# One store or two per 128-row output tile in place of four, in a memory-attention and two-layer kernel

## The chip, the cores and the metric

The kernel runs on one core of a Trainium2 chip. The metric is the device time of the whole program in microseconds, as the median of the timed runs of the same kernel on the same inputs. Smaller is better.

## The reference

Attention against 32 memory rows per head, then a gated layer, then a layer with a sigmoid-weighted activation. What is cut is only the random inputs.

```python
def _attn_ref(q, k, v, phi):            # q, k, v: (4, 8, 576, 64); phi: (4, 8, 576, 32)
    a = softmax of phi over the sequence
    k_m = np.einsum('bhsm,bhsd->bhmd', a, k)
    v_m = np.einsum('bhsm,bhsd->bhmd', a, v)
    attn = softmax of scale * q @ k_m.T over the memory rows
    return attn @ v_m

x = attn_out.transpose(0, 2, 1, 3).reshape(2304, 512)
x = ((x @ w_a) * (x @ w_b)) @ w_out              # d_ff 1536
h = x @ w_in                                     # d_ff 2048
return (h * (1.0 / (1.0 + np.exp(-1.702 * h)))) @ w_out2     # (2304, 512) float32
```

## The kernel before

The 2304 tokens are 4 batches of 576. A small planner (`Order`, L67 to L143) runs generators in an order that it works out from estimated costs, and each generator issues its instructions when it is resumed; the order on each engine is thereby fixed when the program is built. It plans TensorE, VectorE, ScalarE and GpSimd. Transfers that are issued from SyncE are not planned: they stand in SyncE's queue in the order in which the generators reach them.

Within a batch the tokens are held in a permuted order. A block is 32 tokens (`QP`), and a batch has 18 blocks (`QC`). The rows of the batch are seen as 32 groups of 18 consecutive rows; a block holds one row out of each group, so the 32 rows of a block stand 18 rows apart in memory. The first nine blocks of a batch (288 tokens, half a batch) hold the even rows of the groups, the last nine the odd rows. Row c of an even half is row 2c of each group.

The tail of the kernel is the second layer. `main` (L860) runs over eight groups of 256 hidden columns, and within a group over six units of 384 tokens: `gelu` (L773) makes the hidden values of a unit, `proj2` (L817) multiplies them into three tiles of 128 tokens by 512 output columns, 6 matmuls (L828) a tile. `proj2_out` (L838) adds a tile into `acc` in SBUF on VectorE (L844). In the last group it then calls `store` (L806) for the tile. A tile has four blocks; `store` goes over them one by one and issues one transfer a block on SyncE: 32 partitions of `acc` to 32 rows of the output, 2 KB each, 18 rows apart. 18 tiles of four blocks make 72 transfers (L815). Nothing writes a tile of `acc` after its store, and no later instruction but the end of the program waits for a store.

The half batch has nine blocks and a tile has four, so a tile can begin at any of the nine blocks, and some tiles reach over the end of a half.

Of the kernel before, what the change touches and what calls it, by code (L numbers as in the profile page):

```python
# [146 lines left out]
def tile_mem_attention_moe_moe2(  # L147
# [13 lines left out]
    nc = tc.nc  # L161

    w_a, w_b, w_o1, w_in, w_o2 = (w.bitcast(U32) for w in (w_a, w_b, w_o1, w_in, w_o2))
    B, H, S, D = q.shape
# [4 lines left out]
    P = 128  # L169
# [5 lines left out]
    QP = P // 4  # L175
    QC = S // QP
# [629 lines left out]
    def store(i, src):  # L806

        for t in range(i * P, (i + 1) * P, QP):
            b, r = divmod(t, S)
            e, c = divmod(r // QP, QC // 2)
            dst = out[b * S:(b + 1) * S, :].rearrange("(p c) e -> p c e", c=QC)
            nc.sync.dma_start(out=dst[:, 2 * c + e, :], in_=src[t - i * P:t - i * P + QP, :])  # L815

    def proj2(g, i):  # L817
        t0 = yield from weights("o2", g)
# [19 lines left out]
    def proj2_out(t, g, it, ps):  # L838
        dst = acc_o[:, it, :]
        t, _ = yield DVE, t, dve(512)  # L840
        if g == 0:
            nc.vector.tensor_copy(dst, ps[0])
        else:
            nc.vector.tensor_tensor(out=dst, in0=ps[0], in1=dst, op=ALU.add)  # L844
        bank_m.release(ps, t)
        if g == NG2 - 1:
            store(it, dst)
# [81 lines left out]
    with tc.manual_schedule():  # L929
# [15 lines left out]
        for n in range(NU):  # L945
            p = 10 + n if n >= NHG else 10 + PC * n
# [42 lines left out]
```

## Time and profile before

| | us |
|---|---|
| median of three timed runs | 832.27 |
| lowest and highest of them | 831.84, 833.02 |
| the profiled execution's own time | 829.86 |
| its span, from the first to the last instruction | 828.1 |
| TensorE busy | 808.0 |
| VectorE busy | 565.3 |
| ScalarE busy | 363.4 |
| GpSimd busy | 319.8 |

All rows come from one profiled execution. Its engines are PE (TensorE matmul), PEld (its weight loads), DVE (VectorE), ACT (ScalarE) and POOL (GpSimd); SPq is the queue of SyncE, which here only issues transfers. A transfer is made of packets that 16 DMA engines carry; a share of DMA is the mean busy share of these 16. The span is 1.76 us shorter than that execution's own time, and that time is 2.41 us under the median of the timed runs.

### The profile page before, as it was taken

The numbers are of one execution on the slowest core, as the hardware profiler recorded it, in microseconds if no ns is written. First come the engines' busy times: TensorE is split into PE (matmuls) and PEld (weight loads), VectorE is DVE, ScalarE is ACT, GpSimd is POOL, SyncE is SP. The second block draws the span as 40 slices with busy tenths as digits, with TensorE's granted clock in tenths as the row PEclk, the third lists the DMA queues.
The fourth block names the chain that finished last, engine by engine and source line by source line (L and its number), as shares of the span: only waits on it lengthen the run. The fifth ranks groups of instructions, "written<-read, shape, count | busy, mean of one in ns | idle before, by whom it ended". The sixth has DMA issues, their size and how long they took to land.

```text
span 828.1 us, 13746 instructions
## 1 busy us (share of the span) xinstructions
PE 808.0 (98%) x5290; PEld 743.5 (90%) x5290; DVE 565.3 (68%) x1020; ACT 363.4 (44%) x795; POOL 319.8 (39%) x294
## 2 busy tenths in 40 slices
PE   8999999999999999999999999999999999999996
PEld 7777788989999999999999899989898989999995
DVE  4988879997977969858498664846557384444342
ACT  4567777454445536436553333324233242322220
POOL 1212255643524426326675433424334161322120
PEclk9999999999999999999999999999999999999999
DMA  8866402240310301301022110201103000000134
GB/s 301 296 208 186 145 1 77 82 149 2 104 50 27 102 26 52 104 1 51 1 74 80 48 55 0 82 21 52 51 1 102 1 26 1 1 0 1 33 87 110
DMA packets 33025, 57.77 MB, mean 70 GB/s; under 512 B 3520, under 2 KB 15808, under 8 KB 32960
## 3 DMA queue, kind: packets, MB, share of 16 engines
q1 hardware_dynamic: 32128, 56.08, 21.6%
q10 hardware_dynamic: 832, 0.82, 0.3%
q8 instruction: 41, 0.67, 0.3%
q14 instruction: 24, 0.20, 0.1%
HBM read 52.17 MB, written 4.72 MB: 69 GB/s over the span
## 4 chain that ended last, share of the span: by engine, by line
PE 79%; DVE 10%; ACT 4%; issue 3%; DMA 2%; POOL 0%; SPq 0%; DVEq 0%; ACTq 0%
PE bank L828 23%; PE bank L787 22%; PE bank L731 13%; PE bank L698 13%; PE bank L659 2%; DVE dm L351 2%; DVE dm L347 1%; DMA raw<-in_moe_w_b_dram 1%; DVE dm L356 1%; PE bank L491 1%; PE bank L631 1%; DVE gr L714 1%; PE bank L531 1%; DVE acc L748 1%; PE bank L406 1%
## 5 line engine op out<-in xcount | busy, mean ns | idle before, releaser
L828 PE MATMUL bank<-wo,g 128*128 128x512 f32 x864 | 204.6, 390 | 0.2 <-POOL g L253 0.2
L253 POOL TENSOR_TENSOR g<-sg,g 128x384 fp32r<-128x384 f32 x95 | 102.8, 1084 | 226.9 <-ACT g L259 180.2
L828 PEld LDWEIGHTS bank<-wo,g 128*128 128x128 f32 x864 | 161.5, 188 | 31.5 <-POOL g L253 0.6
L800 DVE TENSOR_TENSOR sg<-bank,sg 128x384 f32<-128x384 f32 x96 | 53.4, 556 | 115.2 <-ACT sg L798 115.2
L798 ACT ACTIVATE sg<-bank 128x384 f32<-128x384 f32 x96 | 47.0, 489 | 177.7 <-PE bank L787 177.4
L844 DVE TENSOR_TENSOR acc<-bank,acc 128x512 f32<-128x512 f32 x126 | 86.8, 689 | 51.4 <-PE bank L828 51.3
L253 POOL TENSOR_TENSOR g<-gr,g 128x288 fp32r<-128x288 f32 x74 | 64.0, 867 | 135.5 <-ACT g L259 128.9
L787 PE MATMUL bank<-y,whl_b 128*128 128x384 f32 x576 | 105.0, 337 | 0.0
L787 PE MATMUL bank<-y,whl_a 128*128 128x384 f32 x576 | 104.2, 336 | 0.5 <-DVE sg L800 0.5
L787 PEld LDWEIGHTS bank<-y,whl_b 128*128 128x128 f32 x576 | 101.7, 188 | 1.9
L787 PEld LDWEIGHTS bank<-y,whl_a 128*128 128x128 f32 x576 | 100.7, 188 | 2.5 <-DVE sg L800 0.9
L731 PE MATMUL bank<-g,whl_a 128*128 128x288 f32 x576 | 82.9, 298 | 0.9 <-DVE gr L714 0.7
L731 PEld LDWEIGHTS bank<-g,whl_a 128*128 128x128 f32 x576 | 78.3, 189 | 5.3 <-issue 3.5
L731 PE MATMUL bank<-g,whl_b 128*128 128x288 f32 x576 | 80.1, 296 | 1.0 <-ACT gr L711 1.0
L731 PEld LDWEIGHTS bank<-g,whl_b 128*128 128x128 f32 x576 | 77.8, 188 | 2.0 <-ACT gr L711 1.2
L259 ACT ACTIVATE g<-sg 128x384 fp32r<-128x384 f32 x96 | 50.6, 527 | 65.7 <-DVE sg L800 65.3
L748 DVE TENSOR_TENSOR acc<-bank,acc 128x288 f32<-128x288 f32 x160 | 68.2, 450 | 14.5 <-PE bank L731 13.9
L259 ACT ACTIVATE g<-gr 128x288 fp32r<-128x288 f32 x96 | 42.6, 443 | 67.0 <-DVE gr L714 66.9
L343 POOL TENSOR_SCALAR dm<-dm 128x512 f32<-128x512 f32 x32 | 53.3, 1667 | 34.2 <-ACT dm L341 34.2
L714 DVE TENSOR_TENSOR gr<-bank,gr 128x288 f32<-128x288 f32 x96 | 43.4, 452 | 28.4 <-PE bank L698 22.7
L711 ACT ACTIVATE gr<-bank 128x288 f32<-128x288 f32 x96 | 38.4, 400 | 45.4 <-PE bank L698 45.0
L698 PE MATMUL bank<-attn,eff 128*128 128x288 f32 x384 | 56.0, 302 | 1.9 <-ACT acc L245 1.9
(118 smaller groups left out, 1120.5 us busy)
## 6 DMA issues: line engine op xcount, KB each, us to landing
raw<-in_moe_w_out_dram SPq DMA_DIRECT2D x28, 512.0 KB, 3.7
raw<-in_moe_w_in_dram SPq DMA_DIRECT2D x16, 512.0 KB, 3.6
raw<-in_moe_w_a_dram SPq DMA_DIRECT2D x22, 256.0 KB, 2.8
raw<-in_moe_w_b_dram SPq DMA_DIRECT2D x22, 256.0 KB, 3.1
q<-in_q_dram SPq DMA_DIRECT2D x8, 576.0 KB, 6.6
out_dram<-acc SPq DMA_DIRECT2D x72, 64.0 KB, 1.7
kv<-in_k_dram SPq DMA_DIRECT2D x8, 320.0 KB, 4.6
kv<-in_v_dram SPq DMA_DIRECT2D x8, 320.0 KB, 5.8
```

Source lines behind the costliest of these rows:

```text
L253: (nc.gpsimd if e == POOL else nc.vector).tensor_tensor(out=dst, in0=in0, in1=in1, op=op)
L259: nc.scalar.activation(out=hi, in_=src, func=AF.Copy)
L343: (nc.vector if e == DVE else nc.gpsimd).tensor_scalar(out=mf, in0=mf, scalar1=2.0 ** -15, scalar2=None, op0=ALU.max)
L698: nc.tensor.matmul(ps[0][:, :U], e[:, c, sw, i * CW + j * P:i * CW + (j + 1) * P], attn(b, mv, c, u * U, U), start=(n == 0), stop=(n == 3 ...
L714: nc.vector.tensor_tensor(out=gr[0], in0=pb[0][:, :U], in1=gr[0], op=ALU.mult)
L731: nc.tensor.matmul(ps[0][:, :U], w[:, sw, j, mb * P:(mb + 1) * P], g1[0][:, j, mv, :], start=(n == 0), stop=(n == 3 * G1 - 1),)
L748: nc.vector.tensor_tensor(out=dst, in0=ps[0][:, :U], in1=dst, op=ALU.add)
L787: nc.tensor.matmul(ps[0][:, :N2], w[:, sw, c, j * P:(j + 1) * P], yhl[half, mv][:, c, o:o + N2], start=(n == 0), stop=(n == 3 * KD - 1),)
L798: nc.scalar.activation(out=sg[0], in_=ps[0][:, :N2], func=AF.Sigmoid, scale=1.702)
L800: nc.vector.tensor_tensor(out=sg[0], in0=ps[0][:, :N2], in1=sg[0], op=ALU.mult)
L828: nc.tensor.matmul(ps[0], g2[0][:, j, sw, s * P:(s + 1) * P], w[:, mv, j, :], start=(n == 0), stop=(n == 3 * G2 - 1),)
L844: nc.vector.tensor_tensor(out=dst, in0=ps[0], in1=dst, op=ALU.add)
```

## The change

`store` no longer issues one transfer for each block. It takes as many consecutive blocks as lie both in the tile and in the same half batch, and stores them in one transfer. The source is then n x 32 partitions of `acc`; the destination is n blocks, two rows apart, of 32 rows each, 18 rows apart. A tile that lies in one half batch is stored in one transfer of four blocks, a tile that reaches over the end of a half in two. Nothing else in the kernel is touched.

```diff
-        for t in range(i * P, (i + 1) * P, QP):
+        t = i * P
+        while t < (i + 1) * P:
             b, r = divmod(t, S)
             e, c = divmod(r // QP, QC // 2)
-            dst = out[b * S:(b + 1) * S, :].rearrange("(p c) e -> p c e", c=QC)
-            nc.sync.dma_start(out=dst[:, 2 * c + e, :], in_=src[t - i * P:t - i * P + QP, :])
+
+            n = min(QC // 2 - c, ((i + 1) * P - t) // QP)
+            rows_ = out[b * S:(b + 1) * S, :].rearrange("(p c e) f -> e c p f", c=QC // 2, e=2)
+            nc.sync.dma_start(
+                out=rows_[e, c:c + n], in_=src[t - i * P:t - i * P + n * QP, :]
+            )
+            t += n * QP
```

## Rows read from the trace of the kernel before

**Rows 1.** The page: the span, busy time by engine, shares of the last chain.
```profile
span 828.1 us, 13746 instructions
...
PE 808.0 (98%) x5290; PEld 743.5 (90%) x5290; DVE 565.3 (68%) x1020; ACT 363.4 (44%) x795; POOL 319.8 (39%) x294
...
PE 79%; DVE 10%; ACT 4%; issue 3%; DMA 2%; POOL 0%; SPq 0%; DVEq 0%; ACTq 0%
```

**Rows 2.** Line L815, the stores: ns min/median/max, first and last start; time to landing.
```profile
L815 SPq DMA_DIRECT2D out_dram<-acc x72: 314/425/652, 781.1 to 825.1; - x72
...
DMA to landing us min/median/max: 1.6/1.7/1.9
```

**Rows 3.** Chain of waits from 780 us: start, us, engine and line.
```profile
791.36 4.24 PE bank L787 x24
795.60 4.08 PE bank L828 x18
...
812.24 8.17 PE bank L828 x36
820.41 0.02 issue
820.43 0.69 DVE acc L844
```

**Rows 4.** Timeline of VectorE: start, us, what, and the idle time before it.
```profile
780.36 0.69 DVE L844 TENSOR_TENSOR acc<-bank,acc 128x512 f32<-128x512 f32 x1 [0.25 <-PE bank L828]
...
788.66 0.69 DVE L844 TENSOR_TENSOR acc<-bank,acc 128x512 f32<-128x512 f32 x1 [0.25 <-PE bank L828]
```

**Rows 5.** Timeline from 820 us: start, us, engine, line, what.
```profile
819.95 5.55 SPq L815 DMA_DIRECT2D out_dram<-acc  x12
```

**Rows 6.** Waits of SyncE's queue: us in total, times, longest.
```profile
SPq L984 <- DMA out_dram<-acc: 1.3, 1, 1.3
```

**Rows 7.** DMA view, 781 to 789 us, then 814.4 to 827.5 us.
```profile
DMA packets 576, 0.79 MB, mean 98 GB/s; under 512 B 192, under 2 KB 192, under 8 KB 576
q1 hardware_dynamic: 576, 0.79, 39.5%
...
out_dram<-acc SPq DMA_DIRECT2D x12, 64.0 KB, 1.7
...
DMA packets 1152, 1.57 MB, mean 120 GB/s; under 512 B 384, under 2 KB 384, under 8 KB 1152
...
q1 hardware_dynamic: 1152, 1.57, 48.7%
...
out_dram<-acc SPq DMA_DIRECT2D x24, 64.0 KB, 1.7
```

**Rows 8.** Busy time by stretch; last columns: granted TensorE clock, DMA share, GB/s.
```profile
20.00:36.00 16.00, 15.19 (x162) 11.97 (x162) 14.16 (x35) 9.05 (x23) 5.06 (x6) 1.00 1.02 377
...
814.40:827.50 13.10, 6.00 (x27) 4.64 (x25) 3.46 (x5) 0.00 (x0) 0.72 (x1) 0.93 0.49 120
```

**Rows 9.** The page, part 3: packets, MB and share of SyncE's transfer queue.
```profile
q1 hardware_dynamic: 32128, 56.08, 21.6%
```

## The prediction

> **What bounds the kernel now.** I read the page first: the span is 828.1 us, TensorE is busy 98% of it, and the chain that ended last gives TensorE 79% and DMA 2% [rows 1]. So nothing in the body of the kernel waits for stores; a change to stores can act only where they run. The first store starts at 781.1 us and the last at 825.1 us [rows 2], so I read the last 47 us alone. Their chain of waits is TensorE without a break, rounds of 24 matmuls (4.24 us) and 18 matmuls (4.1 us), until the last add on VectorE, which starts at 820.43 us and takes 0.69 us [rows 3]. The arithmetic is therefore done at 821.1 us, and 7.0 us of span follow. What fills them is the SyncE queue: each of the 72 stores occupies it for a median of 425 ns [rows 2], so a tile's four take 4 x 0.425 = 1.7 us, while in the last 36 matmuls (8.17 us, six tiles [rows 3]) a tile is finished every 1.36 us. The queue falls behind: from 819.95 us to 825.5 us it only issues, 12 stores without a gap [rows 5]. The last store is issued at 825.1 us, lands 1.7 us later [rows 2] at 826.8 us, which is the 1.3 us that SyncE waits for it at the end [rows 6], and 828.1 - 826.8 = 1.3 us close the span.
>
> The second thing to see is what the DMA engines do with a store. 24 stores appear as 1152 packets, 384 of them under 512 B [rows 7]: per store 32 packets, one for each 2 KB row, and 16 small ones. The first 12 stores, of three tiles, show the same: 576 packets, 192 of them small [rows 7]. I read the 16 as one closing packet from each of 16 engines, so today each engine carries two rows of a store.
>
> **What is removed.** 72 issues become 24: per batch half of nine 32-row blocks the tiles are cut into blocks of 4, 4, 1+3, 4, 2+2, 4, 3+1, 4, 4, and this repeats once. That is 12 stores of four blocks, 4 of three, 4 of two, 4 of one. Of 72 x 0.425 = 30.6 us of issuing 20.4 us go. All but the backlog at the end is hidden under TensorE [rows 3]. The last tile is one store (four blocks), which can be issued at 821.15 us instead of 825.1 us: 3.9 us of the path go, if nothing else changes. No compute instruction is added, moved or made to wait; the stores read tiles that nothing writes again, and no load is left in this stretch: all packets of queue q1 there are accounted for by the stores [rows 7]. So TensorE, VectorE, ScalarE and GpSimd keep their times.
>
> **What is added.** The bytes and the 2 KB rows stay, 2304 packets in all, but the shape changes. Before, a store's destination was one run of 32 equal steps (18 rows apart). After, a destination of n blocks is two loops, n outside and 32 inside, against one run of 32n partitions at the source. No row of the trace shows a transfer with an outer loop of less than 32, so its cost is bounded from both sides. At one end the engines deal the rows as before, and a 128-row store takes 128/16 = 8 packets on each engine. At the other end they are dealt along the outer loop, one block to an engine: n engines, 32 packets on each. I take the second: blocks lie 2 rows apart and the rows in a block 18, so that the two loops cannot be written as one run of 32n steps, and whoever deals out equal shares along one loop has the outer one to deal. I also take the same engines each time, as no row shows a choosing. [...]
>
> Then the first engine carries 32 packets of each of the 20 stores with several blocks and 2 of each of the 4 single ones: 648 packets. The price of one packet: the stores of the last stretch keep 0.49 of 16 engines busy for 120 GB/s, 120/(0.49 x 16) = 15.3 GB/s an engine, 2048 B in 133 ns; the loads early on run at 377 GB/s and 1.02, 23.1 GB/s an engine, 89 ns [rows 8]. The slow price is that of 16 engines crowded into 32 partitions, the fast one that of 16 engines over all 128. After, each engine has 32 partitions to itself, which is nearer to the load's spread; but two of four engines may meet. I take 100 ns, a quarter of the way up, and keep 89 and 133 as the ends.
>
> **The sum.** The queue of the first engine does not run dry: three tiles arrive every 8.3 us (adds at 780.36 and 788.66 us [rows 4]), and they bring 98, 128 or 98 packets, 9.8 us or more at 100 ns, 8.7 us even at 89 ns. So the end is the start plus the work. The first issue is at 781.1 us; of its 1.7 us to landing [rows 2] two packets of 133 ns are transfer, 1.4 us are fixed; then 648 packets; then the 1.3 us that close the span. 781.1 + 1.4 + 64.8 + 1.3 = 848.6 us against 828.1, that is +20.5 us. The profiled execution took 829.86 us, 1.8 us more than its span, and the median of the timed runs is 832.27, 2.4 us above that; I add the difference to the median: 852.8 us. At 89 ns it is 57.7 us of packets, +13.4, 845.7 us; at 133 ns 86.2 us, +41.9, 874.2 us. The freed SyncE time is worth nothing in this case: the last issue stands 26 us ahead of the landing.
>
> **The rivals.**
> *Spread over 16 engines (faster).* The last store is issued at 821.15 us, needs 1.4 us and 8 packets of 133 ns, 1.06 us, lands at 823.6 and the span ends at 824.9 us: -3.2 us, 829.1 us. For it: every transfer of the trace closes on 16 engines [rows 7]. Against: none of them has a short outer loop. The point from which it decides is 16 pieces out of n x 32 rows. 0.12.
> *Four engines, but a different four each time (no change).* Then nothing piles up, and only the last store counts: 821.15 + 1.4 + 32 x 0.1 + 1.3 = 827.1 us at 100 ns, 828.1 at 133: -1.0 to 0, 831.3 to 832.3 us. For it: nothing in the rows says which engines take a transfer; against: 16 of 16 in use never needed a choice. 0.05.
> *The same few engines, and two of them in each other's way (slower still).* The engines of one store start together and walk their blocks in step; if they meet as the 16 do now, a packet costs 133 ns throughout, 874.2 us. For it: the 133 ns of [rows 8] are already a price of meeting. Against: a single-block store between, and a store that starts on other blocks, moves them out of step. 0.25. [...]
>
> **How the numbers follow.** The forecast, the same few engines at 89 to 110 ns, has 0.58, its slow rival 0.25, no change 0.05, faster 0.12. The predicted time is 852.8 us. The two slow cases hold 0.83; the range takes both of them, 845.7 to 874.2, widened by 3 us below and 5 us above for the order in which the engines pick up queued stores and the cost between two stores on an engine, which no row prices: 843 to 879 us. Left out are the faster case, the unchanged one and some 0.03 above. Times within 0.2%, 1.7 us, can't be told from no change: faster 0.12, same 0.05, slower 0.83.
>
> **What would show it.** Packets first: the small closing packets of the 72 stores are 1152 now; with n engines a store they become 12 x 4 + 4 x 3 + 4 x 2 + 4 x 16 = 132, so queue q1 falls from 32128 packets [rows 9] to 31108; spread over 16 it would be 24 x 16 = 384 and 31360. Then the rate: after 782 us some 70 GB/s without pause instead of bursts of 120 and more [rows 7, 8], and it goes on for 20 us or more after VectorE's last add, which still starts near 820.4 us. SyncE's wait at the end grows from 1.3 us [rows 6] to over 20, and the time from issue to landing from 1.7 us [rows 2] to many times that in the later stores, while the number of issues is 24. If the wait at the end stays near 2.5 us and the last issue stands near 821 us, the stores were spread and I am wrong in the dealing; if the stores are few-engined but the end is far from 849 us, the price of a packet was wrong, and the share of the engines against the rate gives it. If the last add moves, something I held to be independent was not.

## The result and the profile after

The changed kernel takes 842.29 us in the median (840.55 to 842.58), the kernel before, beside it, 832.06 us (830.82 to 833.02). The ratio is 1.0129, with a 95% interval from 1.0117 to 1.0141: 10.2 us slower. The direction and the mechanism came out as forecast, the size did not: 20.5 us were forecast, and 842.29 lies just under the low end of the range, 843.

The page of the changed kernel, taken of its execution of 840.55 us: span, busy time by engine, and part 3, packets, MB and share of SyncE's queue.

```profile
span 838.7 us, 13696 instructions
...
PE 807.2 (96%) x5290; PEld 743.0 (89%) x5290; DVE 565.6 (67%) x1020; ACT 362.5 (43%) x795; POOL 318.0 (38%) x294
...
q1 hardware_dynamic: 31108, 56.08, 21.3%
```

The span grew from 828.1 to 838.7 us, and no engine has over 0.3 us more to do than in [rows 1]. The packets of q1 fell from 32128 [rows 9] by 1020, to the very number that stores carried by n engines would leave, 31108; stores on 16 engines would have left 31360.

The stores (ns min/median/max, first and last start), the end of the chain of waits, and SyncE's waits (us in total, times, longest):

```profile
L818 SPq DMA_DIRECT2D out_dram<-acc x24: 321/564/2465, 780.9 to 824.9; - x24
...
812.09 8.17 PE bank L834 x36
820.26 0.02 issue
820.29 0.69 DVE acc L850
...
SPq L990 <- DMA out_dram<-acc: 11.0, 1, 11.0
```

The arithmetic ends where it did, at 821.0 us against 821.1 [rows 3]. Between that and the end of the span there are now 17.7 us in place of 7.0. SyncE waits 11.0 us at the end for stores to land; it was 1.3 [rows 6]. The 24 issues are there, but the longest takes 2465 ns where the longest before took 652 [rows 2]; more on that below.

Busy time by stretch (us, the five engines, granted TensorE clock, DMA share, GB/s), while the arithmetic runs and after it:

```profile
806.00:814.00 8.00, 8.00 (x43) 7.34 (x42) 3.01 (x5) 2.03 (x4) 1.71 (x3) 1.00 0.31 100
...
822.00:830.00 8.00, 0.00 (x0) 0.00 (x0) 0.00 (x0) 0.00 (x0) 0.00 (x0) 0.64 0.28 94
833.00:835.00 2.00, 0.00 (x0) 0.00 (x0) 0.00 (x0) 0.00 (x0) 0.00 (x0) 0.50 0.13 51
```

Compare with [rows 8]: in the first two stretches the stores now run at 94 to 100 GB/s, with a share of some 0.3 of the 16 engines, and they go on after the arithmetic. At the end 0.13 of 16, that is 2.1 engines, carry 51 GB/s: 24.5 GB/s an engine, 84 ns for 2 KB by the share, and 25.5 GB/s or 80 ns if it is two engines exactly. In the prediction the price of such a packet was 100 ns.

### The profile page after: what moved, and what is told of

It reads as the page before. It is cut to its first block, busy times and chain, and to the rows that moved or that the text cites. A ratio compares the mean times of both kernels' runs of the same rounds, so it can differ in the third digit from the quotient of the medians.

```text
span 838.7 us, 13696 instructions
## 1 busy us (share of the span) xinstructions
PE 807.2 (96%) x5290; PEld 743.0 (89%) x5290; DVE 565.6 (67%) x1020; ACT 362.5 (43%) x795; POOL 318.0 (38%) x294
## 3 DMA queue, kind: packets, MB, share of 16 engines
q1 hardware_dynamic: 31108, 56.08, 21.3%
## 4 chain that ended last, share of the span: by engine, by line
PE 79%; DVE 10%; ACT 4%; issue 3%; DMA 2%; POOL 0%; SPq 0%; DVEq 0%; ACTq 0%
PE bank L834 22%; PE bank L787 22%; PE bank L731 14%; PE bank L698 13%; PE bank L659 2%; DVE dm L351 2%; PE bank L491 1%; DVE dm L347 1%; PE bank L531 1%; DVE dm L356 1%; PE bank L631 1%; DVE gr L714 1%; PE bank L406 1%; DVE acc L748 1%; DVE dm L343 1%
```

## The experiments

Each kernel was timed beside the kernel before on the same chip; the change is given against that. In these rounds the kernel before had medians of 830.1 to 830.9 us, lower than the 832.06 above, so kernels are compared by the ratio. The short diffs are against the changed kernel, where nothing else is said; `...` marks what is left out. The theory under test: a store whose destination has an outer loop of n blocks is carried by n engines, always the same first ones; these fall behind, and what is still queued on them when the arithmetic ends is the loss.

**Stores of two blocks at most.** A dealing by the outer loop would make smaller stores worse, since by it 32 packets fall to the first engine for two blocks as for four.

```diff
-            n = min(QC // 2 - c, ((i + 1) * P - t) // QP)
+            n = min(2, QC // 2 - c, ((i + 1) * P - t) // QP)
```

> No store takes more than two blocks: 32 stores of two blocks and 8 of one, 40 in all. Theory (a store of n blocks is carried by n engines, always the same first ones): the first engine has 32 x 32 + 8 x 2 = 1040 packets; at the 84 ns that two engines showed at the end of the changed kernel (0.13 of 16 engines, 51 GB/s) that is 87.4 us after 782.3, the span ends near 871, the time is +43, 875 us; small packets 32 x 2 + 8 x 16 = 192. Rival 1 (the engines rotate, or the cost goes with the bytes of a store): smaller stores cost less than the changed kernel's, 832 to 836 us. Rival 2 (two engines in step are in each other's way): these two work alone on blocks 32 partitions apart; at 133 ns a packet it is 138 us, 926 us.

Measured: 871.87 us, ratio 1.0507 [1.0492, 1.0523], +42 us against +43 expected. The stretch after the arithmetic, and part 3 of the page:

```profile
834.00:836.00 2.00, 0.00 (x0) 0.00 (x0) 0.00 (x0) 0.00 (x0) 0.00 (x0) 0.50 0.13 51
840.00:842.00 2.00, 0.00 (x0) 0.00 (x0) 0.00 (x0) 0.00 (x0) 0.00 (x0) 0.50 0.13 51
...
q1 hardware_dynamic: 31168, 56.08, 20.4%
```

Two engines, 51 GB/s, as at the end of the changed kernel. Packets are 31168, and 32128 - 1152 + 192 is 31168. With stores of half the size the loss is four times that of the changed kernel. If the engines rotated, or the cost followed the bytes, this kernel would stand near 834 us: the first rival falls. The second did not come about: two engines that walk blocks 32 partitions apart needed no more than 84 ns a packet here, not 133. It was put to the test only in part, as no view shows the two in step; the section on the prediction has the times of the changed kernel.

**Only the first nine tiles stored as in the change.**

```diff
-            n = min(QC // 2 - c, ((i + 1) * P - t) // QP)
+            n = min(QC // 2 - c, ((i + 1) * P - t) // QP) if i < 9 else 1
```

> The first nine tiles are stored as in the changed kernel (12 stores), the last nine block by block (36). Theory (only what is still queued on the first engines when the arithmetic ends costs time): 324 packets x 84 ns = 27.2 us after 782.3, done by 809.5, before the last tiles' stores from 814 us on; the end is that of the kernel before, 832 us within 1. Rival (each combined store costs a fixed amount wherever it stands): half of +10, 837 us.

Measured: 829.85 us beside 830.09, ratio 0.9998 [0.9988, 1.0008]. A dozen of the changed stores cost nothing where the first engines have time to finish before the end. The loss is the queue that is left, not a price a store.

**Only the last tile stored as in the change.**

```diff
-            n = min(QC // 2 - c, ((i + 1) * P - t) // QP)
+            n = min(QC // 2 - c, ((i + 1) * P - t) // QP) if i == NT // P - 1 else 1
```

> Only the last tile is stored in one transfer of four blocks, the others block by block. It measures one such store with nothing queued before it. Theory (four engines, 32 packets each): SyncE reaches it at 823.7 us, 1.4 us fixed and 32 x 84 ns = 2.7 us, landing 827.8, span 829.1 against 828.1: +1.0, 833.0 us. Rival (spread over 16 engines when nothing is queued): 1.4 + 8 x 0.133 = 2.5, span 827.5: -0.6, 831.4 us.

Measured: 832.56 us, ratio 1.0030 [1.0020, 1.0041], +2.5 us where +1.0 was expected. The store is dealt to four engines, as the theory has it: q1 has 32068 packets, 60 fewer than before, so one store went from 64 closing packets to 4. But this single store takes longer than the fixed part and 32 packets together. Part 3 of the page, the last issue on SyncE (start, us), SyncE's wait at the end, and two stretches (last columns DMA share, GB/s):

```profile
q1 hardware_dynamic: 32068, 56.08, 21.8%
...
823.04 0.69 SPq L818 DMA_DIRECT2D out_dram<-acc  x1
...
SPq L990 <- DMA out_dram<-acc: 5.0, 1, 5.0
...
825.00:826.00 1.00, 0.00 (x0) 0.00 (x0) 0.00 (x0) 0.00 (x0) 0.00 (x0) 0.50 0.20 20
826.00:828.00 2.00, 0.00 (x0) 0.00 (x0) 0.00 (x0) 0.00 (x0) 0.00 (x0) 0.50 0.25 89
```

From issue to landing it is 0.69 + 5.0 = 5.7 us; 1.4 us fixed and 32 packets of 84 ns make 4.1. From 825 to 826 us four engines are not idle (a share of 0.20 is 3.2 of them) and yet move only 20 GB/s; then four (0.25) run at 89 GB/s. So the start of this store has a slow stretch worth some 1.6 us. What causes it was not tried.

**The same 24 stores, written as one run.** The tokens of each half batch are put in the order of the output's rows, so that any piece of a tile is a run of rows two apart. The order is made in the copy of the transposed queries. `U` is half a batch, 288 tokens, and `j` counts the tokens in it.

```diff
-                qT[0][:, :, c0 * QP:(c0 + k) * QP].rearrange("p h (c s) -> p c h s", s=QP),
+                qT[0].rearrange("p h (s c) -> p c h s", c=QC // 2)[:, c0:c0 + k],
...
+            n = min(U - j, (i + 1) * P - t)
+            rows_ = out[b * S:(b + 1) * S, :].rearrange("(j e) f -> e j f", e=2)
+            nc.sync.dma_start(out=rows_[e, j:j + n], in_=src[t - i * P:t - i * P + n, :])
...
```

> 24 stores as in the changed kernel, but the tokens of a half batch are put in the order of the output's rows (in the copy of the transposed queries), so that a store is one run of 128 (or 32, 64, 96) equal steps of two rows. Theory (the outer loop decides): 16 engines a store, 24 x 16 = 384 small packets, nothing piles up; the last store is issued at 821.15, 1.4 us and 8 packets of 89 to 133 ns, landing 823.3 to 823.6, span 824.6 to 824.9: -3.2 to -3.5, 828.7 us. The packets near 89 ns if 16 engines crowded into 32 partitions made the 133, near 133 if it was 16 engines writing at once. Rival (a large store is slow by its size): as the changed kernel, 842 us. The copy writes 36 bytes apart; if that is slow the early part grows by some us.

Measured: 830.98 us, ratio 1.0013 [1.0003, 1.0023]. The 10 us that the changed kernel lost are gone with the same sizes of store, so a store is not slow for its size; but the 3 us that were to be gained did not come. The last add, SyncE's wait, part 3 of the page; then ScalarE's copies of the transposed queries, of the kernel before and of this one (busy us, mean ns):

```profile
825.54 0.69 DVE acc L847
...
SPq L987 <- DMA out_dram<-acc: 1.7, 1, 1.7
...
q1 hardware_dynamic: 31360, 56.08, 21.3%
```

```profile
L245 ACT ACTIVATE qT<-bank 128x512 f32<-128x512 f32 x16 | 9.5, 598 | 1.8 <-PE bank L406 1.6
```

```profile
L245 ACT ACTIVATE qT<-bank 128x512 f32<-128x512 f32 x16 | 17.8, 1127 | 1.9 <-PE bank L406 1.7
```

31360 packets: 16 engines a store. The last add ends at 826.2 us and the span, 829.4 us, 3.2 us later, against 7.0 before: the stores gain 3.8 us. But the last add comes 5.1 us late. The copies write 36 bytes apart and take 1127 ns in place of 598; that they are what makes the add late is argued, not shown.

**Two queues.** The kernel before (the diff is against it), with every second store of the last three tiles issued from ScalarE.

```diff
+            odd = i >= NT // P - 3 and t // QP % 2
+            (nc.scalar if odd else nc.sync).dma_start(
...
```

> The stores of the kernel before, but of the last three tiles every second block is issued from ScalarE's queue. It asks whether the end before was set by the issuing on one queue, and so what the change could have gained. Theory: SyncE issues the 12 stores of tiles 12 to 14 by 819.6 us and two of each later tile; the last issue starts near 821.8 instead of 825.1, lands 1.7 us later, the span ends near 824.8: -3.3 us against the kernel before. Rival (the DMA engines, not the issuing, set the end): no change.

Measured: 832.97 us beside 830.93, ratio 1.0024 [1.0015, 1.0033]. SyncE's waits:

```profile
SPq L816 <- DMA out_dram<-acc: 4.9, 1, 4.9
```

SyncE stood 4.9 us for another store to land: in the trace of the kernel before the stores signal their landing through eight semaphores in turn, numbers 102 to 109, and an issue waits for the earlier store on its own semaphore. Here that was one of ScalarE's queue: SyncE issued nothing from 817.7 to 822.55 us, while ScalarE issued stores from 819.55 us on. The experiment put in a wait that it was not meant to have, and doesn't answer its question; the kernels before and after it do.

**The order made late.** Stores as in the one-run kernel; the order is made where the first layer's result is split for the second.

```diff
+        hi, lo = (yhl[half, i][:, kb, o:o + n].rearrange("p k (s c) -> p k s c", s=QP) for i in (HI, LO))
+        src = acc_y[:, half, kb, o:o + n].rearrange("p k (c s) -> p k s c", s=QP)
...
```

> Stores as in e4_one_run (24, one run of equal steps each, 16 engines), but the tokens are put in that order where the first layer's result is split for the second (ScalarE reads and the difference reads 128 bytes apart, both write contiguously), and the copy of the transposed queries is that of the kernel before. Theory: e4_one_run lost 5.1 us before the last add to copies of 1127 ns in place of 598; without these the last add ends near 821.1 us as before, and the span 3.2 us after it as there: 824.3, -3.8 us. Rival (the order costs wherever it is made): the 24 splits delay the second layer's start by some us, 0 to +3. Stores of 128 rows near 86 ns a packet; of 64 rows near 150 as of 32, if what slows packets is how few parts of SBUF 16 engines read, near 86 if it is only 32 rows that are slow.

Measured: 830.55 us beside 830.93, ratio 0.9996 [0.9987, 1.0005]: the rival. The end after the last add is 3.1 us, but the last add comes 3.5 us late; the splits on ScalarE that read 128 bytes apart take 1295 ns in place of 676, and TensorE is 2.7 us less busy between 300 and 480 us; that the splits cause this is argued, as above. What it shows of the packets, in a stretch with stores of 128 rows only and one with stores of 64 rows:

```profile
785.40:788.20 2.80, 2.80 (x17) 2.60 (x16) 1.26 (x2) 0.00 (x0) 0.00 (x0) 1.00 0.50 188
795.10:796.30 1.20, 1.20 (x8) 1.20 (x8) 0.53 (x1) 0.00 (x0) 0.00 (x0) 1.00 0.59 135
```

128 rows: 188/(0.50 x 16) = 23.5 GB/s an engine, 87 ns. 64 rows: 135/(0.59 x 16) = 14.3 GB/s, 143 ns, as slow as the 32-row stores of the kernel before. So the 133 ns of [rows 8] are no price of storing as such: 16 engines pay 133 to 143 ns where a store reads 32 or 64 partitions, and 87 where it reads 128.

**Fewer issues at the end, in the old order.**

```diff
-            n = min(QC // 2 - c, ((i + 1) * P - t) // QP)
+            n = min(QC // 2 - c, ((i + 1) * P - t) // QP) if i < 9 or i in (12, 14) else 1
```

> Token order as in the kernel before. Tiles 0 to 8, 12 and 14 are stored as in the changed kernel, the others block by block: 18 issues instead of 24 after 814 us, and only two four-block stores near the end, whose 5.7 us each (e3_last_only, issue to landing) are over by about 820 and 823 us. Theory (the end is set by SyncE's issuing and by whatever is still queued on the first engines): SyncE reaches the last block at about 823.3 instead of 825.1 us, the time is 1.8 us under that of the kernel before. Rival (the stores of the last tiles have to queue behind the two large ones on the first four engines): no gain, or up to 1 us more.

Measured: 831.44 us beside 830.59, ratio 1.0009 [0.9997, 1.0021]: no gain, as the rival says. SyncE's waits:

```profile
SPq L818 <- DMA out_dram<-acc: 4.1, 3, 2.2
```

SyncE saved six issues and lost 4.1 us in three waits for stores to land; the last issue starts at 826.5 us. As in the two-queue kernel, a late store held up the issue that shares its semaphore, here by 2.2 us at most.

**The order made by the load.** Stores as in the one-run kernel; the queries come in pieces of 512 B, four loads a unit.

```diff
-                src = q[b, g * HG:(g + 1) * HG].rearrange("h (p c) d -> (h p) (c d)", c=QC)
-                nc.sync.dma_start(out=s[0].rearrange("p c d -> p (c d)"), in_=src)
+                for h in range(HG):
+                    src = q[b, g * HG + h].rearrange("(c p e) d -> p c (e d)", p=QP, e=2)
+                    dst = s[0][h * QP:(h + 1) * QP].rearrange("p (c e) d -> p c (e d)", e=2)
+                    nc.sync.dma_start(out=dst, in_=src)
```

> Stores as in e4_one_run and e7_late_order (24, one run of equal steps, 16 engines), but the tokens come in that order by the load of the queries: each of the 8 loads becomes 4, one a head, in pieces of 512 B instead of 4608 B. No compute instruction differs from the kernel before. Theory: the end after the last add shrinks from 7.0 to 3.2 us as in those two; the loads of small pieces take up to 0.7 us more for each of the first two units and 3 more issues of 0.43 us each, so the last add comes 0 to 2 us later; 2 to 4 us under the kernel before, 827 to 829 us. Rival (as in the two others, the order costs what the stores gain): no change.

Measured: 828.87 us beside 830.58, ratio 0.9974 [0.9959, 0.9989]: faster. The end after the last add is 3.2 us, and the last add still 3.6 us later than in the kernel before, where 0 to 2 us were expected. The 0.7 us a unit in the expectation were the author's estimate, and no run shows them: a load of 144 KB in pieces took 6.7 us from issue to landing in the median, a load of 576 KB in the kernel before 6.6.

**The same for all batches but the first.** The first batch keeps its load and its stores block by block; its tiles are stored long before the end.

```diff
+                if b == 0:
...
+                for h in range(HG if b else 0):
```

> As e9_q_pieces, but the first batch keeps the loads of the kernel before (4608 B pieces, one a unit) and is stored block by block (18 stores); the other three batches are loaded in pieces of 512 B and stored in runs of equal steps (18 stores). In e9_q_pieces the last add came 3.6 us later than in the kernel before, with TensorE 3.1 us less busy in the first 80 us. Theory (that loss is the first batch waiting for its queries, the other batches' loads are hidden): the last add returns to about 821.1 us and the end stays 3.2 us after it: -3.8 us, 826.8 us. Rival (the loads of the later batches or the extra issues on SyncE cost it): as e9_q_pieces, 828.9 us.

Measured: 826.81 us beside 830.69, ratio 0.9952 [0.9936, 0.9967]; 826.8 was expected. The first 80 us of the kernel with all batches in pieces, then of this one; this one's last add and its span:

```profile
0.00:80.00 80.00, 70.78 (x749) 57.41 (x749) 58.46 (x143) 46.22 (x121) 15.95 (x25) 1.00 0.92 245
```

```profile
0.00:80.00 80.00, 74.03 (x805) 60.34 (x806) 61.49 (x150) 48.62 (x126) 16.78 (x26) 1.00 0.87 248
...
820.57 0.69 DVE acc L856
...
span 824.3 us, 13727 instructions
```

TensorE's work in the first 80 us is back (73.88 us before), the last add ends at 821.3 us, and the span ends 3.0 us after it. This kernel beats both. It has 36 stores, 18 of them still block by block; what gains some 4 us is that the stores of the other three batches, the last ones among them, are runs that 16 engines share.

## Why the prediction was right and where it was wrong

- *What bounds the end before.* Right. With fewer stores, all on 16 engines, the end shrinks from 7.0 us to 3.0 to 3.2 in four kernels, three of them with 24 stores and the last with 36. And before the change no store took over 1.9 us to land [rows 2], so the DMA engines were not behind. The forecast for that case was 3.2 us less; it is about 3.8.
- *The dealing along the outer loop, and the same engines each time.* Right: 31108 packets after, and 42 us lost with two blocks a store. The closing packets of the stores are as many as this dealing gives in each kernel: 132 for stores of 4, 3, 2 and 1 blocks, 192 with pairs, 384 with one run. More than four blocks were not tried. The rivals "spread over 16" and "a different four each time" are out.
- *The 648 packets of the first engine.* Right as a count, and the second engine has 648 too, which is why two are left at the end. That the queue never runs dry holds as well: the trace has at least two packets in flight at every moment from 782.3 to 836.7 us. But it held by less than the prediction thought. It had 8.7 us of work or more, even at 89 ns, for every 8.3 us; at 84 ns the 98 packets of two groups in three take 8.2 us, and only the 128 of the third, with the slow starts, keep a backlog.
- *The price of a packet.* This is the step that failed. I took 100 ns, a quarter of the way from the loads' 89 to the stores' 133 [rows 8], and held 89 for the low end. Measured: 80 to 84 ns. In the prediction's own sum, with the first issue at 780.9 us, 648 x 84 ns give 780.9 + 1.4 + 54.4 + 1.3 = 838.0 us of span, 838.7 was measured; with 80 ns it is 835.4, and the rest is about twice the slow start of a single store. Taken whole, the term measured 838.7 - 780.9 - 1.4 - 1.3 = 55.1 us where 64.8 were forecast, 85 ns a packet with the slow starts in it. Of the forecast's 20.5 us, 648 x 16 ns = 10.4 us were this term. The rows that I went between were both prices of 16 engines at once: the store's of 16 engines that read 32 partitions, the load's of a time at which all 16 were full (a share of 1.02). Neither was taken where two to four engines work, as they do after the change; why those needed less is not shown. With 84 ns for the low end the range would have begun near 839 us and held the result.
- *The rival "two of them in each other's way".* It did not come about: in the two-block kernel the two engines that work alone needed 84 ns at most. That does not refute it, because no view shows its condition met. Each engine ends its share of a store with a closing packet, and the trace of the changed kernel has these at 834.12 and 834.76 us and again at 836.69 and 837.33 us. So its last two engines run 0.64 us apart, by an estimate at 80 ns a packet eight rows, and are not in step; for the two-block kernel no view shows whether they were. What put them out of step was not tried, and what a packet costs two engines in step no run shows. What the runs have of crowding is the price of 16 engines: 143 ns where a store reads 64 partitions, 87 where it reads 128.
- *The marks.* SyncE's wait at the end was to pass 20 us; it is 11.0. I had put the last issue at 821 us, 26 us ahead of its landing. SyncE did not run that far ahead: its issues themselves took up to 2465 ns, and the last stands at 824.9. That moved the mark, not the end. The rate was to be some 70 GB/s; the stretches above have 94 to 100, and 51 with two engines left.

## What to carry to other kernels

Before merging transfers, write the merged one as loops and look at the outermost count on either side: here a count of 2, 3 or 4 meant that so few DMA engines carried the transfer (132 closing packets in place of 1152), and always the same ones, so that the work of all merged transfers piled up there (10.2 us lost, 42 with pairs). Merge only what is one run of equal steps over many partitions. The runs had 87 ns a packet where 16 engines read 128 partitions, 133 to 143 where they read 32 or 64. If the layout doesn't allow it, try to change it where the data comes in: here that gained 1.7 us with all batches and 3.9 with all but the first (TensorE busy 74.03 us of the first 80, against 70.78 with all), while the two orders made on a compute engine gained nothing. A pile-up in the middle of the kernel, with the first nine tiles merged, cost nothing here (a ratio of 0.9998), as it was gone at the end; so price one by what is still queued when the last result is ready.

## What was not expected of the hardware

- SyncE was held inside its issues while the engines were far behind: they took a median of 2266 ns in the two-block kernel and up to 2465 ns in the changed one, where 425 ns was the median before [rows 2]. It is not a wait for a semaphore: SyncE's waits in the changed kernel have none for a store but the last one. In both kernels the last store landed 11.0 to 11.1 us after its issue had ended, which at 80 to 84 ns is an estimate of some 130 to 140 packets on the first engine that SyncE's queue was ahead.

```profile
L818 SPq DMA_DIRECT2D out_dram<-acc x40: 414/2266/4431, 780.8 to 854.4; - x40
...
SPq L990 <- DMA out_dram<-acc: 11.1, 1, 11.1
```

- The four-block store of the last tile, on idle engines, spent about a microsecond at 20 GB/s before it reached 89. The first store of the changed kernel started as slowly, at 14 GB/s:

```profile
782.50:783.70 1.20, 1.20 (x8) 1.14 (x7) 0.69 (x1) 0.00 (x0) 0.00 (x0) 1.00 0.26 14
```

- ScalarE took about twice as long where it wrote 36 bytes apart (1127 ns against 598, copies of 128x512) or read 128 bytes apart (1295 against 676, splits of 128x576).
